# A convolution through two Fourier steps: two pieces of filler work are placed in later half rounds

## The chip, the cores and the metric

The kernel runs on one core of a Trainium2 chip. A core has five engines that work side by side, each through its own queue in program order: TensorE (PE in the profile; matmuls, with PEld for its weight loads), VectorE (DVE), ScalarE (ACT), GpSimd (POOL) and SyncE (SP), which issues the DMAs. Matmuls write into PSUM, eight banks; VectorE and ScalarE carry results from there into SBUF. The metric is the device time of one execution in microseconds (us).

## The reference

```python
# x: (1, 224, 224, 96) bf16, w: (7, 7, 96, 96) bf16
wp = jnp.pad(w, ((0, H - K), (0, W - K), (0, 0), (0, 0)))
Xf = rfft2(x.astype(float32), axes=(1, 2))
Wf = rfft2(wp.astype(float32), axes=(0, 1))
Yf = jnp.einsum('bhwi,hwio->bhwo', Xf, Wf)
y = irfft2(Yf, s=(H, W)).astype(bfloat16)
```

It is a circular 7 x 7 convolution of a 224 x 224 image with 96 channels in and 96 out, written as a product of spectra.

## The kernel before

**What it computes.** The kernel transforms only along the rows' axis h, in 8 blocks of 28 rows that overlap by 6, to 17 frequencies per block (`NS`, slots 0 to 16; slots 0 and 16 hold real parts only). Along the other axis w it stays in the pixel domain and forms two output pixels at a time from fewer products than a plain sum over taps would take.

**Tiles.** The image is cut along w into seven tiles of 32 columns, `t` = 0 to 6 in the code. The third tile is `t` = 2; below, "tile 2" means this. For each tile four kinds of work follow each other:

- the forward transform: matmuls of pixels (`xn`) with a table (`Fm`) into a PSUM bank, and an evacuation into `xf`. There are two such buffers, so tile 2 uses tile 0's again. A copy of three neighbour columns per phase from the previous tile goes before it (`new_xf`, line 432; two ScalarE copies).
- planes: sums and differences of `xf` on VectorE, into `J` (`jit`, line 518), for groups of three slots (`JGB`), three instructions per group.
- rounds: one per slot (`b_round`, line 578). The first product, 19 matmuls into one bank, uses `J` and `xf` as weights' side and the transformed filter `WF`; ScalarE copies a part of it (`tt_`), VectorE forms `u` from the bank and that copy. Then a place for filler work, `mid()`. The second product, 14 matmuls into another bank, from which VectorE forms `v`. GpSimd (in some rounds VectorE) adds u and v into `yf`. Then a second place for filler work, `end()`. The buffers of u and v are two each, so the u of a round waits until GpSimd has added the one of two rounds before. In slots 0 and 16 a round has 8 + 14 matmuls and one VectorE sum.
- the inverse transform: `yf` goes to DRAM (`scr`), comes back in another order (`tt`, `load_t`, line 702), and an inverse job (`c_jobs`, line 762) multiplies it with `Gm`: two matmuls into two banks, two evacuations into `yo` or a free plane buffer, and the output DMA after some of the jobs. A tile has eleven such jobs, on five loads. When a load's last job is done, the next load into its buffer is issued (`pump`).

**Order.** Every engine's order is the order in which the Python code emits the work. Filler work stands in lists: `add(a, b, jobs)` (line 853) spreads jobs evenly over half rounds a to b - 1, and `pace` (line 837) emits as many of them at a `mid()` or `end()` as are due:

```python
due = n if k >= b - 1 else -(-n * (k - a + 1) // (b - a))
while jobs and n - len(jobs) < due:
    jobs.pop(0)()
```

**Tiles 0 and 1** run together, tile 1 four rounds behind tile 0 (line 869, `r` = 0 to 20). While both run (r = 4 to 16), half round 2r is tile 0's round and half round 2r + 1 is tile 1's. Fillers here: filter jobs (`prep_jobs`, line 388: matmuls on `wq` into a bank, evacuated into `WF` by ScalarE, and at the end of each group the differences of `WF` on VectorE), with the last group in half rounds 22 to 26; and tile 2's forward transform in two ranges of slots (`FR2`, line 44; lines 886 to 893): slots 0 to 9 from half round 22 in nine half rounds, 12 jobs (one bank, 5 or 6 matmuls and one evacuation each), and slots 10 to 16 from half round 34 in six, 8 jobs. At the end of the second range the pixels of tile 3 are loaded.

**Tiles 2 to 6** run one by one (line 923). Here half rounds 2s and 2s + 1 are the `mid()` and `end()` of round s. Fillers of tile t: the forward transform of tile t + 1 (24 jobs up to half round 25) and inverse jobs of tile t - 1 or what is left of tile t - 2. In tile 2 these are the eleven jobs of tile 0 (`CQ[2] = (11, 0)`), paced from half round `k0` (line 933) to 33; in the other tiles they start in half round 3. The loads for tile 0's inverse jobs are queued in round r = 20 of the stretch before.

**PSUM.** All banks come from one pool of eight. A bank that a matmul wants must have been emptied by the VectorE or ScalarE instruction that reads it; which bank that is follows from the order of the program. An evacuation goes to VectorE or ScalarE by a running count of each one's load (`evac`); from tile 0's rounds on this puts nearly all of them on ScalarE.

Of the kernel before, what the change touches and what calls it, by code (L numbers as in the profile page):

```python
# [40 lines left out]
CQ = {2: (11, 0), 3: (11, 2), 4: (9, 5), 5: (6, 8), 6: (3, 8)}  # L41
SH2 = (0, 8, 13, 17)
FR0 = (0, 8, 17)
FR2 = ((0, 10, 22, 9), (10, 17, 34, 6))
MERGE = ()
NP2 = 0
FI = 6
# [11 lines left out]
def kernel(  # L59
# [426 lines left out]
    def a_jobs(t):  # L486
        xf = new_xf(t)
        jobs = []
        for jg in range(2):
            for h in range(2):  # L490
                for (q, n) in ((0, 3), (3, 3), (6, 2)):
                    jobs.extend(a_bank(t, xf, xn_bufs[jg], h * PXC + 2 * q, n, jg, HALO + h * 8 + q))
            jobs.append(then_load(jobs.pop(), t + 1, jg))
        return jobs
# [23 lines left out]
    def jit(t, g):  # L518
        s0, s1 = JGB[g]
        n = s1 - s0  # L520
        xf = xf_tiles[t][0:C]
        xv = xf.rearrange("c p r s w j -> c p r s (w j)")
        b = jcount[0] % 3 if t < 2 else (jcount[0] - 2 * len(JGB)) % 2
        jcount[0] += 1
        Jb = J_bufs[b][0:C].rearrange("c (k s q) -> c k s q", k=7, s=3)
        for s in range(s0, s1):
            jbuf[(t, s)] = Jb[:, :, s - s0]

        def sub(o, a, b, op, cost):
            def f():  # L530
                load["v"] += 170 + cost / 1.92
                return VE.tensor_tensor(out=o, in0=a, in1=b, op=op)
            return f
        x0, x1 = xv[:, 0, :, s0:s1], xv[:, 1, :, s0:s1]
        c0, c1 = max(s0, REAL[0] + 1), min(s1, REAL[1])
        i0, i1 = c0 - s0, c1 - s0
        pd, rd, sd, qd = x1.ap
        dpl = bass.AP(x1.tensor, x1.offset - NJ, [pd, [NJ, 2], rd, sd, qd])
        return [
            sub(Jb[:, 0:4, 0:n].rearrange("c (k r) s q -> c k r s q", r=2), dpl,  # L540
                x0.unsqueeze(1).to_broadcast([C, 2, 2, n, PP]), ALU.subtract, 4 * PP * n),
            sub(Jb[:, 4, i0:i1], xv[:, 0, 0, c0:c1], xv[:, 0, 1, c0:c1], ALU.add, PP * (c1 - c0)),
            sub(Jb[:, 5:7, i0:i1], Jb[:, 0:4:2, i0:i1], Jb[:, 1:4:2, i0:i1], ALU.add, 2 * PP * (c1 - c0)),
        ]

    def late_planes(s):
        x0, x1 = (xf_tiles[TL][0:C, ph, :, s].rearrange("c r w j -> c r (w j)") for ph in range(2))
        o = LATE[s]
        Jb = jbuf[(TL, s)] = xs[0:C, o:o + 7 * PP].rearrange("c (k q) -> c k q", q=PP)
        pd, rd, qd = x1.ap  # L550
        dpl = bass.AP(x1.tensor, x1.offset - NJ, [pd, [NJ, 2], rd, qd])

        def sub(o, a, b, op, n):
            def f():
                load["v"] += 170 + n * PP / 1.92
                return VE.tensor_tensor(out=o, in0=a, in1=b, op=op)
            return f
        ops = [sub(Jb[:, 0:4].rearrange("c (k r) q -> c k r q", r=2), dpl, x0.unsqueeze(1).to_broadcast([C, 2, 2, PP]), ALU.subtract, 4)]
        if s not in REAL:
            ops += [sub(Jb[:, 4], x0[:, 0], x0[:, 1], ALU.add, 1), sub(Jb[:, 5:7], Jb[:, 0:4:2], Jb[:, 1:4:2], ALU.add, 2)]  # L560
        return ops
# [167 lines left out]
    def turn_a(i):  # L729
        src = xn_all[:, 0:NA].bitcast(F32).rearrange("p (g k s) -> p g k s", k=2, s=SR)  # L730
        turn(src, xs[:, 0:NA], i * C // 8, (i + 1) * C // 8)
# [30 lines left out]
    def c_jobs(t):  # L762
        jobs = []
        w0 = t * 2 * TW
        for gi, h in LT:
            hold = {}
            nq = 2 if gi < 2 else 3

            def mk_(q, gi=gi, h=h, nq=nq, hold=hold):
                def put(j0, nj, px, npx, row, col):  # L770
                    dma(out[0, j0 * B:(j0 + nj) * B, w0 + px:w0 + px + npx, :].rearrange("h w c -> h (w c)"),
                        hold["yo"][row:row + nj * B, col:col + npx * C])

                def f():
                    if q % 2 == 0:
                        hold["yo"] = new_yo()
                    tt = tt_tiles[(t, gi, h)]
                    yo = hold["yo"]
                    nj = 2 if q == 2 else 3
                    for b in range(2):  # L780
                        pb = bank()[0:3 * B, 0:4 * C]
                        TE.matmul(pb, lhsT=G[0:nj * FR],
                                  rhs=tt[0:nj * FR, 4 * q + 2 * b:4 * q + 2 * b + 2, :].rearrange("p w e -> p (w e)"), start=True, stop=True)
                        k = 2 * (q % 2) + b
                        evac(yo[0:nj * B, k * 4 * C:(k + 1) * 4 * C], pb[0:nj * B], 4 * C)
                    if q == 1 and gi < 2:
                        put(gi * 3, 3, h * PXC, PXC, 0, 0)
                    elif q == 1:
                        put(6, 2, 0, 16, 0, 0)
                        for j in range(2):  # L790
                            put(6 + j, 1, 24, 8, 2 * B, j * 8 * C)
                    elif q == 2:
                        put(6, 2, 16, 8, 0, 0)
                    if q == nq - 1:
                        held[gi == 2] -= 1
                        pump()
                return f
            for q in range(nq):
                jobs.append(mk_(q))
        return jobs  # L800
# [11 lines left out]
    def queue_c(t):  # L812
        pend.extend((t, *k) for k in LT)
        pump()
# [30 lines left out]
    def fills(qs, k):  # L845
        def f():
            for q in qs:
                pace(q, k)
        return f
# [3 lines left out]
    def add(a, b, jobs):  # L853
        qs.append([a, b, jobs, len(jobs)])
# [14 lines left out]
    for r in range(NS + LAG):  # L869
# [5 lines left out]
        for p in range(3):  # L875
            if r == (1, 3, 5)[p]:
# [8 lines left out]
                add(2 * r + 1, 2 * r + (5, 5, 4)[p], fj[0] + fj[1])  # L885
        for s0, s1, k0, n in FR2:
            if 2 * r == k0:
# [35 lines left out]
    for t in range(2, NT):  # L923
        if t == TL:
            GE.memset(YA[:, :, 2 * SA:, :].rearrange("p g s o -> p g (s o)"), 0.0)
        else:
            scr_tiles[t] = dr_pool.tile([TW, NJ, NS, 4 * C], BF16, name="scr")
        qs = []
        if t + 1 < NT:
            add(4 if t == 2 else 0, 26, a_jobs(t + 1))  # L930
        nold, nnew = CQ[t]
        k1 = 2 * NS if t < TL else 2 * NS - 2
        k0 = 10 if t == 2 else 3
        km = 14 if t == TL else k0 + -(-(k1 - k0) * nold // (nold + nnew))
        add(k0, km, cj[:nold])
        cn = c_jobs(t - 1)
        cj = cn[nnew:]
        add(km, k1, cn[:nnew])
        plan = {}
        for g, (s0, s1) in enumerate(JGB):  # L940
            if g + 1 < len(JGB) - (t == TL) or t + 1 < NT:
                plan[s0 if g + 1 < len(JGB) else s0 - 1] = g
        for s in range(NS):
            now = ()
            if s in plan:
                g = plan[s]
                now = jit(t, g + 1) if g + 1 < len(JGB) else jit(t + 1, 0)
            if s == 3:
                queue_c(t - 1)
            if t in (3, 4):  # L950
                next(gp, None)
            mid = fills(qs, 2 * s)
            if t == TL and s in LROUND:
                now = late_planes(LROUND[s])
            if t == TL and s >= SA:
                if s < NS - 1:
                    now = [lambda i=s - SA: turn_a(i)]
                else:
                    mid = lambda m=mid: (m(), turn_a(3))
            b_round(t, s, mid, fills(qs, 2 * s + 1), bool(now) and t != TL, now)  # L960
# [70 lines left out]
```

## Time and profile before

| | |
|---|---|
| median of 3 runs | 257.67 us (257.16 to 257.9) |
| the profiled execution | 257.39 us, span 255.7 us |
| granted TensorE clock | 0.998 |
| TensorE busy | 245.9 us (96%), 5015 matmuls |
| VectorE busy | 214.5 us (84%) |
| ScalarE busy | 201.6 us (79%) |
| GpSimd busy | 108.4 us (42%) |
| chain that ended last | TensorE 82%, DMA 7%, VectorE 4% |

All instructions carry line 92, the helper that records the order, so rows are told apart by tiles: `pb<-WF,J` and `pb<-WF,xf` are products, `pb<-wq` filter jobs, `pb<-Fm,xn` forward transforms (80 columns per matmul in tile 2's first range, 56 in its second, 136 in later tiles), `pb<-tt,Gm` inverse jobs. A row of a timeline gives the start in us, the duration in us, the engine and line, the operation, its tiles, and in brackets the idle time of the engine before it with what ended that. Rows of equal instructions are merged; the end of a row of matmuls is modelled and overlaps the next row, so starts are the better measure. Tile 0 and 1's rounds end near 92 us, tile 2's at 121, tile 3's at 152.

### The profile page before, as it was taken

To read this page: it belongs to the slowest core of one execution; us is meant where nothing else is said; L and a number is where in the kernel's file an instruction comes from. 1 tells how busy PE (TensorE), PEld (TensorE's weight loads), DVE (VectorE), ACT (ScalarE), POOL (GpSimd) and SP (SyncE) were. 2 spreads that over 40 slices of the span, in tenths; PEclk is the share of its full clock that TensorE was granted. 3 is DMA by queue.
4 is the path that set the end of the run, shared out by engine and by line. 5 is a ranking of instruction groups with operands and counts; after the bars stand their busy time and mean duration, and the time that the engine had idled before them with its cause. 6 is when DMAs were issued, how large, how long until landed. Compare 5 with 4: busy or idle time off the path is not lost.

```text
span 255.7 us, 11925 instructions
## 1 busy us (share of the span) xinstructions
PE 245.9 (96%) x5015; PEld 231.5 (91%) x5015; DVE 214.5 (84%) x463; ACT 201.6 (79%) x499; POOL 108.4 (42%) x174
## 2 busy tenths in 40 slices
PE   8989999999999999999999999999999999999981
PEld 3789999999999998999999989999999999999971
DVE  6999899899788987779788896788978889989982
ACT  7889978586973877997988879888897976567762
POOL 7885514354446535331433324433243332464721
PEclk9999999999999999999999999999999999999999
DMA  7963103711111569887989559697959853496145
GB/s 170 244 184 93 43 9 91 233 49 49 49 49 53 175 187 158 241 234 233 283 247 227 168 154 313 195 271 189 322 209 207 258 169 104 137 172 177 54 121 178
DMA packets 41511, 42.80 MB, mean 167 GB/s; under 512 B 30836, under 2 KB 33072, under 8 KB 41458
## 3 DMA queue, kind: packets, MB, share of 16 engines
q1 hardware_dynamic: 41140, 41.36, 58.5%
q8 instruction: 39, 0.64, 1.0%
q0 software_dynamic: 192, 0.52, 0.7%
q10 hardware_dynamic: 126, 0.17, 0.2%
q14 instruction: 14, 0.11, 0.1%
HBM read 22.37 MB, written 19.66 MB: 164 GB/s over the span
## 4 chain that ended last, share of the span: by engine, by line
PE 82%; DMA 7%; DVE 4%; issue 2%; ACT 2%; SPq 1%; POOL 0%; DVEq 0%
PE pb L92 82%; DMA tt<-scr 2%; DMA WF<-in_x_dram 2%; DMA wq<-in_w_dram 2%; SPq L92 1%; ACT xf L92 1%; DVE xf L92 1%; DVE J L92 1%; DVE WF L92 1%; DVE v L92 1%; DVE u L92 0%; POOL yf L92 0%; ACT tt L92 0%; ACT WF L92 0%; ACT ct L92 0%
## 5 line engine op out<-in xcount | busy, mean ns | idle before, releaser
L92 PE MATMUL pb<-WF,J 96*128 96x96 bf16 x2782 | 160.3, 206 | 0.5 <-DVE u L92 0.4
L92 PEld LDWEIGHTS <-J 96*128 96x128 bf16 x2782 | 136.8, 98 | 7.3 <-issue 0.7
L92 POOL TENSOR_TENSOR yf<-v,u 128x384 bf16<-128x384 f32 x70 | 69.6, 1010 | 119.3 <-issue 64.1
L92 ACT CAST xf<-pb 96x408 bf16<-96x408 f32 (+8 forms) x145 | 67.5, 488 | 3.9 <-PE pb L92 1.8
L92 PE MATMUL pb<-WF,xf 96*128 96x96 bf16 x991 | 61.5, 206 | 0.7 <-ACT xf L92 0.4
L92 DVE TENSOR_TENSOR J<-xf 96x1824 bf16<-96x1824 bf16 (+1 forms) x82 | 56.0, 722 | 0.1
L92 PEld LDWEIGHTS <-xf 96*128 96x128 bf16 x991 | 48.9, 98 | 1.4 <-ACT xf L92 0.6
L92 PE MATMUL pb<-Fm,xn 118*128 118x136 bf16 (+5 forms) x576 | 44.4, 203 | 0.0
L92 PE MATMUL pb<-tt,Gm 102*84 102x384 bf16 (+1 forms) x132 | 32.0, 325 | 0.5 <-DMA tt<-scr 0.5
L92 ACT CAST yo<-pb 84x384 bf16<-84x384 f32 (+1 forms) x65 | 27.8, 484 | 3.3 <-PE pb L92 3.3
L92 ACT CAST J<-pb 84x384 bf16<-84x384 f32 (+1 forms) x65 | 28.0, 486 | 2.2 <-PE pb L92 2.2
L92 ACT CAST WF<-pb 96x480 bf16<-96x480 f32 (+1 forms) x59 | 29.0, 562 | 0.7 <-PE pb L92 0.6
L92 PEld LDWEIGHTS <-xn 118*128 118x128 bf16 x576 | 29.0, 97 | 0.3
L92 DVE TENSOR_TENSOR J<-J 96x912 bf16<-96x912 bf16 (+2 forms) x41 | 22.6, 551 | 0.0
L92 PE MATMUL pb<-wq 128*128 128x120 bf16 (+1 forms) x288 | 21.7, 226 | 0.5 <-ACT wq L92 0.5
L92 PEld LDWEIGHTS <-wq 128*128 128x128 bf16 x288 | 19.7, 149 | 1.0 <-ACT wq L92 0.9
L92 POOL TENSOR_TENSOR xn<-v,u 128x384 bf16<-128x384 f32 x12 | 10.9, 923 | 8.9 <-DVE J L92 5.9
L92 PEld LDWEIGHTS <-Gm 102*84 102x84 bf16 (+1 forms) x132 | 11.4, 118 | 0.8 <-issue 0.6
L92 DVE TENSOR_TENSOR yf<-v,u 128x384 bf16<-128x384 f32 x20 | 11.3, 567 | 0.8 <-DMA scr<-yf 0.2
L92 ACT COPY xf<-xf 96x816 bf16<-96x816 bf16 (+4 forms) x16 | 9.9, 675 | 0.0
L92 DVE TENSOR_TENSOR WF<-WF 96x960 bf16<-96x960 bf16 x14 | 9.4, 719 | 0.1
L92 PE MATMUL pb<-wu 128*128 128x512 bf16 x26 | 8.1, 479 | 1.1 <-DVE ct L92 1.1
(410 smaller groups left out, 255.0 us busy)
## 6 DMA issues: line engine op xcount, KB each, us to landing
scr<-yf SPq DMA_DIRECT2D x30, 288.0 KB
xn<-in_x_dram SPq DMA_DIRECT2D x12, 672.0 KB
tt<-scr SPq DMA_DIRECT2D x24, 336.0 KB
out_dram<-yo SPq DMA_DIRECT2D x12, 252.0 KB
out_dram<-J SPq DMA_DIRECT2D x12, 252.0 KB
tt<-scr SPq DMA_DIRECT2D x6, 288.0 KB
scr<-yf SPq DMA_DIRECT2D x6, 192.0 KB
WF<-in_x_dram SPq DMA_DIRECT2D x2, 343.0 KB
```

What stands on the lines that cost most here:

```text
L92: r = fn(*a, **k)
```

## The change

Tile 2's first range (slots 0 to 9) moves from half rounds 22 to 30 into half rounds 24 to 33: the neighbour copies are emitted at r = 12 in place of 11, and the 12 jobs are spread over ten half rounds in place of nine. The eleven inverse jobs in tile 2's rounds are spread over half rounds 12 to 33 in place of 10 to 33. No job is added or taken away.

```diff
-FR2 = ((0, 10, 22, 9), (10, 17, 34, 6))
+FR2 = ((0, 10, 24, 10), (10, 17, 34, 6))
...
         nold, nnew = CQ[t]
         k1 = 2 * NS if t < TL else 2 * NS - 2
-        k0 = 10 if t == 2 else 3
+        k0 = 12 if t == 2 else 3
         km = 14 if t == TL else k0 + -(-(k1 - k0) * nold // (nold + nnew))
         add(k0, km, cj[:nold])
```

In the order of the built program this moves, besides the matmuls on TensorE and their evacuations on ScalarE, some DMA issues on SyncE: the load of tile 4's first pixels goes ahead of the first output DMA and the first reload, and two writes of `yf` to DRAM go ahead of an output. The order of instructions on VectorE and GpSimd is the same as before.

## The prediction

> **What bounds the kernel now.** I read the page's busy shares first, then the chain that ended last, then the timelines of TensorE, VectorE and ScalarE around the places where that chain leaves TensorE.
>
> ```profile
> PE 245.9 (96%) x5015; PEld 231.5 (91%) x5015; DVE 214.5 (84%) x463; ACT 201.6 (79%) x499; POOL 108.4 (42%) x174
> PE 82%; DMA 7%; DVE 4%; issue 2%; ACT 2%; SPq 1%; POOL 0%; DVEq 0%
> ```
>
> TensorE is the bound: only its gaps can be saved, and every new gap costs its full length. In the stretches below matmuls follow each other at a fixed pitch, start to start: 42.5 ns for a product matmul (18 in 0.76 us), 36 ns for an 80-column transform matmul (10 in 0.36), 60 ns for a 136-column one (3 in 0.18), 63 ns for a filter matmul (12 in 0.76). Between 28 us and the last tile the chain leaves TensorE at three places. The timeline of TensorE around the first:
>
> ```profile
> 61.51 0.92 PE L92 MATMUL pb<-wq 128*128 128x120 bf16 x12
> 62.27 0.76 PE L92 MATMUL pb<-Fm,xn 118*128 118x80 bf16 x12
> 62.91 0.93 PE L92 MATMUL pb<-WF,J 96*128 96x96 bf16 x18
> ...
> 65.08 0.34 PE L92 MATMUL pb<-Fm,xn 118*128 118x80 bf16 x5
> 65.81 0.93 PE L92 MATMUL pb<-WF,J 96*128 96x96 bf16 x18 [0.39 <-DVE u L92]
> ```
>
> Half round 22 starts its fills at 61.51, half round 23 at 64.31. Five transform matmuls from 65.08 take 0.18, so TensorE stands from 65.26 to 65.81: 0.55 us (the row's 0.39 counts from a modelled end). Twelve from 62.27 should take 0.43 but take 0.64: another 0.20. The cause is VectorE's queue:
>
> ```profile
> 59.83 2.31 DVE L92 TENSOR_TENSOR WF<-WF 96x960 bf16<-96x960 bf16 x3
> 62.06 0.54 DVE L92 SCALAR_TENSOR_TENSOR v<-tt__1756,pb 128x384 f32<-128x384 f32 x1
> ...
> 63.25 1.70 DVE L92 TENSOR_TENSOR J<-xf 96x1824 bf16<-96x1824 bf16 x2
> 64.87 0.62 DVE L92 TENSOR_TENSOR J<-J 96x912 bf16<-96x912 bf16 x1
> 65.42 0.34 DVE L92 SCALAR_TENSOR_TENSOR u<-pb,tt__1849 128x192 f32<-128x192 f32 x1
> 65.68 0.54 DVE L92 SCALAR_TENSOR_TENSOR v<-tt__1849,pb 128x384 f32<-128x384 f32 x1
> 66.66 0.36 DVE L92 SCALAR_TENSOR_TENSOR u<-pb,tt__1926 128x192 f32<-128x192 f32 x1 [0.44 <-POOL yf L92]
> ```
>
> Three filter differences and a group of planes stand in front of u and v, which empty PSUM banks. Half rounds 22 and 23 take 7 and 6 of the 8 banks (two products, three filter jobs, two and one transform jobs), so TensorE soon needs a bank that VectorE still holds. The second and third place, in the same view of TensorE, with the load from the chain:
>
> ```profile
> 92.87 6.32 DMA tt<-scr
> ```
>
> ```profile
> 98.50 0.34 PE L92 MATMUL pb<-Fm,xn 118*128 118x136 bf16 x3
> 99.32 0.49 PE L92 MATMUL pb<-tt,Gm 102*84 102x384 bf16 x2 [0.48 <-DMA tt<-scr]
> ...
> 151.47 0.76 PE L92 MATMUL pb<-WF,J 96*128 96x96 bf16 x14
> 152.53 0.50 PE L92 MATMUL pb<-WF,xf 96*128 96x96 bf16 x8 [0.30 <-DVE u L92]
> ```
>
> 98.50 plus 0.18 is 98.68, and the next start is 99.32: the first inverse job, in half round 10, waits 0.64 for its load. 151.47 plus 14 x 42.5 ns is 152.06: 0.47 at the border from tile 3 to tile 4. At the border from tile 2 to tile 3 (121.02) there is none.
>
> **Part 1: the transform's first range, half rounds 24 to 33.** No work is added: 64 matmuls and 12 evacuations (12 x 0.45 to 0.5 us) move, with two copies of neighbour columns (1.08 us together, ScalarE, at 60.60). All evacuations stay on ScalarE; VectorE's and GpSimd's order stays as it was. The range issues no DMA; the load of tile 3's pixels hangs on the second range, which stays.
>
> VectorE's times up to u of half round 23 do not depend on the moved work: v(21) ends at 63.32, the planes at 65.49, u(22) at 65.76, v(22) at 66.22, u(23), held by GpSimd, at 67.02. TensorE, from 61.51, by the pitches: filter jobs to 62.27, second product of 22 (0.60) to 62.86, first of 23 (0.81) to 63.67, filter jobs to 64.43, second product to 65.02, first of 24 to 65.83 (its planes are ready at 65.49), filter jobs, the second of which now needs v(22): 66.09 to 66.27, a wait of 0.18; they end at 66.76. The two transform jobs of half round 24 need u(23): at 67.07, a wait of 0.30; to 67.48; second product to 68.08. Half round 25 then needs 0.81 + 0.76 + 0.18 + 0.60: 70.42. Before, it ended at 71.26 (70.66 + 0.60) with 32 transform matmuls done, now with 17; the 15 others cost 0.54 later. Saved: 71.26 - 70.42 - 0.54 = **0.30**.
>
> The cover further on: u(24) must be done by 68.89. ScalarE, which now meets the two copies between the dense half rounds, ends half round 23's three filter evacuations at 66.0, the copies at 67.1, the copy that u(24) reads at 67.4; GpSimd frees u's buffer at 67.6; u(24) ends at 68.0. That leaves 0.9 us, and it is 0.3 earlier than before (68.34). After that VectorE runs ahead, since in the trace of before it idles 3.1 us between 66 and 80 (0.44, 0.50, 0.60, 0.75, 0.44, 0.35), and half rounds 31 to 33, empty of fills until now, hold 4 of the 12 jobs while VectorE works without a pause from 80.16 to 86. They take 3 banks each in place of 2; the last needed early, u(29), ends near 77.9 for a start at 79.4.
>
> Ends: +0.75 if neither wait comes back, -0.61 if the same release still stood in front and the 17 matmuls that covered it (0.61) came on top. As built, the bank that TensorE needs there is a later one and more work stands before it, so I take the worked 0.30.
>
> **Part 2: the first inverse job in half round 12.** Eleven jobs (two matmuls, 0.33 us, and two evacuations, 0.74, each), their output DMAs and the reloads of their buffers start two half rounds later and go at every second half round in place of every 2.18. Half round 10 loses its 0.33 and the wait. The second product of half round 10 starts at 99.65 - 0.33 - 0.64 = 98.68; it, the transform job, the next first product and another transform job (0.60 + 0.18 + 0.81 + 0.18) end at 100.45, less part 1's 0.30 at 100.15. There the job of half round 12 finds a load that landed at 99.2, 0.9 us before, or 1.2 if it comes 0.30 earlier as its issue does. Its other two waits, u and v of round 4, end near 99.6 and 100.1. Saved: **0.64** (ends: 0 if the load slipped to 100.8, and 0.64).
>
> [...]
>
> SyncE's queue: tile 4's first pixel loads go ahead of the first output and reload, two writes of the intermediate likewise ahead of an output. Nobody waits for outputs; the reloads serve tile 3, whose first inverse job comes at 124, and were issued from 109.5: over 10 us of cover against a slip of about 2. ScalarE between half rounds 12 and 25, per round: 0.31 + 2.2 x 0.36 + 0.74 = 1.84 us, against TensorE's 1.40 + 0.35 + 0.33 = 2.08: covered by 0.24.
>
> At the end the last jobs move from half rounds 29 and 31 into 28, 30 and 32, the middles of rounds 14 to 16, as tile 3 has them in 30 and 32. As built, the first product of tile 3 then waits for u of round 15, like tile 4's at 152.53. VectorE ends that u 4.0 us after round 14's first product (117.43 to 121.42; 148.48 to 152.47), 4.15 here, since v(14) has to follow the later second product. TensorE gets there after 0.33 + 0.60 + 0.81 + 0.33 + 0.60 + 0.34 + 0.33 + 0.60 = 3.94 (tile 3, one job fewer: 3.58). With 0.06 for the signal: a new wait of about **0.30** (ends: 0, and the 0.59 that tile 4's border loses in all, 0.47 and 0.12 before 152.99).
>
> Sum: 0.30 + 0.64 - 0.30 = 0.64 saved. The profiled execution took 257.39 (span 255.7); it would take 256.75. The median of runs, 0.28 above it, gives 257.67 - 0.64 = **257.03**.
>
> **Rivals.** (a) No wait comes back: 0.30 to 0.75 and 0.64, no loss at the border: 0.94 to 1.39, 256.28 to 256.73. For it: ScalarE and VectorE both run earlier through the dense half rounds. Against it: the program's bank waits at the border.
> (b) The waits only move: part 1 gives 0, the border costs 0.59, and 0.05 is left: 257.62; without the load's gain 258.3. For it: VectorE's queue is unchanged, and it is what TensorE waited for.
> (c) Slower: ScalarE's copies. They stood in a pause of ScalarE (it idles 0.99 before and 1.03 after them) and come to stand behind six evacuations. If u(24) ends later than 68.89, every us is lost by TensorE in full; 1.08 us of copies beyond the 0.9 of cover, with the later jobs shifted behind them, could take up to 1.1, and with part 1 at -0.61: 257.67 + 1.1 + 0.61 + 0.30 - 0.64 = 259.0; near 258.5 where half of it comes. Against it: the rows put u(24) at 68.0. The Trainium skill, "PSUM — Partial Sum Buffer", section "Engine vs sequencer instructions", says that ScalarE's queue is strictly first in, first out, which is how this would come about; the trace agrees, its 499 rows of ScalarE stand in the program's order.
>
> **How the numbers follow.** The forecast (0.3 to 1.0 saved, 256.7 to 257.4) 0.50, (a) 0.20, (b) 0.17, (c) 0.13. 0.3% is 0.77 us, about what can be told from no change: below 256.90 lie (a) and 0.15 of the forecast: 0.35. Above 258.44 lies (c) and little of (b): 0.14. Between: 0.51. The range 256.4 to 258.1 leaves out (c) and the far end of (a).
>
> **What would show it.** Right: no wait at 65.8, two short ones for VectorE near 66.1 and 66.8; no wait for the load near 98.7; a new one for u at tile 3's first product, near 120. Wrong: a wait longer than 0.6 in half rounds 24 or 25, ScalarE as its releaser, or TensorE waiting anywhere between 70 and 83.

## The result and the profile after

The changed kernel takes 256.84 us (median of 22 runs, 256.28 to 257.48), the kernel before, on the same chip, 257.38 (median of 22 runs; the three runs known at the time of the prediction had given 257.67). The ratio is 0.9975, with a 95% interval of 0.9964 to 0.9986: 0.64 us saved of 257.38, between 0.36 and 0.93. The means of the runs (256.80 and 257.45) lie 0.65 apart, the medians 0.54.

The profiled execution of the changed kernel took 257.48 us with a span of 255.8, no less than the one of before (257.39, 255.7). Its half round 22 began at 61.96 in place of 61.51, and what follows tile 4's first product took 0.17 longer (103.32 for 103.15). The change moves no work of TensorE in either stretch, and among the ten profiles shown here half round 22 begins anywhere from 60.97 to 61.96. What the change does is therefore read inside the span, between marks that both profiles have. Busy shares and the chain's shares, from the page:

```profile
PE 246.6 (96%) x5015; PEld 231.7 (91%) x5015; DVE 215.1 (84%) x463; ACT 201.1 (79%) x499; POOL 107.9 (42%) x174
PE 87%; DMA 5%; ACT 2%; issue 2%; DVE 1%; SPq 1%; POOL 0%; DVEq 0%
```

TensorE is as busy as before; its share of the chain went from 82 to 87%, and DMA's from 7 to 5%: the load is off the chain. The chain, in order of time (start, duration, what), now leaves TensorE between 67 us and tile 4 only here:

```profile
67.13 0.37 DVE u L92
67.50 0.04 issue
67.54 53.27 PE pb L92 x1186
...
120.85 0.05 DVE u L92
120.90 0.04 issue
120.94 31.21 PE pb L92 x629
...
152.19 0.21 DVE u L92
```

The timeline of TensorE at the three places where the prediction had something to happen (start, duration, operation; in brackets idle time and what ended it):

```profile
66.31 1.05 PE L92 MATMUL pb<-wq 128*128 128x120 bf16 x12
67.54 0.60 PE L92 MATMUL pb<-Fm,xn 118*128 118x80 bf16 x12 [0.18 <-DVE u L92]
...
69.38 0.96 PE L92 MATMUL pb<-wq 128*128 128x120 bf16 x12
70.18 0.34 PE L92 MATMUL pb<-Fm,xn 118*128 118x80 bf16 x5
70.36 0.93 PE L92 MATMUL pb<-WF,J 96*128 96x96 bf16 x18
...
100.52 0.34 PE L92 MATMUL pb<-Fm,xn 118*128 118x136 bf16 x3
100.70 0.49 PE L92 MATMUL pb<-tt,Gm 102*84 102x384 bf16 x2
...
120.04 0.76 PE L92 MATMUL pb<-WF,J 96*128 96x96 bf16 x14
120.94 0.50 PE L92 MATMUL pb<-WF,xf 96*128 96x96 bf16 x8
```

At half round 24, twelve filter matmuls from 66.31 should end at 67.07, and the transform starts at 67.54: one gap of 0.47 us in place of the two of before, 0.20 and 0.55. The first inverse job starts at 100.70, right behind the three transform matmuls (100.52 plus 0.18): the wait of 0.64 for the load is gone. Tile 3's first product starts at 120.94 where the row ahead of it ends at 120.04 plus 0.60: a new wait of 0.30. VectorE, ScalarE and GpSimd around half round 24:

```profile
63.23 0.53 DVE L92 SCALAR_TENSOR_TENSOR v<-tt__1802,pb 128x384 f32<-128x384 f32 x1
63.70 1.70 DVE L92 TENSOR_TENSOR J<-xf 96x1824 bf16<-96x1824 bf16 x2
65.32 0.62 DVE L92 TENSOR_TENSOR J<-J 96x912 bf16<-96x912 bf16 x1
...
66.14 0.54 DVE L92 SCALAR_TENSOR_TENSOR v<-tt__1847,pb 128x384 f32<-128x384 f32 x1
67.13 0.36 DVE L92 SCALAR_TENSOR_TENSOR u<-pb,tt__1908 128x192 f32<-128x192 f32 x1 [0.46 <-POOL yf L92]
...
68.09 0.36 DVE L92 SCALAR_TENSOR_TENSOR u<-pb,tt__1971 128x192 f32<-128x192 f32 x1
```

```profile
66.44 1.13 ACT L92 COPY xf<-xf 96x480 bf16<-96x480 bf16 x2
```

```profile
63.12 1.01 POOL L92 TENSOR_TENSOR yf<-v,u 128x384 bf16<-128x384 f32 x1 [2.20 <-DVE v L92]
66.08 1.02 POOL L92 TENSOR_TENSOR yf<-v,u 128x384 bf16<-128x384 f32 x1 [1.95 <-issue]
67.07 1.00 POOL L92 TENSOR_TENSOR yf<-v,u 128x384 bf16<-128x384 f32 x1
```

With the 0.45 us by which this profile runs late taken off, u of half round 23 ends at 67.04 (predicted 67.02), ScalarE's copies at 67.12 (67.1) and u of half round 24 at 68.00 (68.0).

Three stretches of TensorE, start to start, serve for all comparisons below: A from the first filter job of half round 22 to the start of half round 34 (0.81 us, a first product, ahead of the first 56-column transform row), B from there to tile 3's first product, C from there to tile 4's first product. C, which nine of the ten kernels leave alone, is 31.50 or 31.51 in all nine.

| kernel | A | B | C | sum | ratio of times to before, 95% |
|---|---|---|---|---|---|
| before | 21.67 | 37.84 | 31.51 | 91.02 | 1 |
| the changed kernel | 21.47 | 37.51 | 31.50 | 90.48 | 0.9975 (0.9964 to 0.9986) |
| part 1 alone | 21.44 | 37.86 | 31.50 | 90.80 | 0.9985 (0.9969 to 1.0002) |
| part 2 alone | 21.69 | 37.70 | 31.50 | 90.89 | 0.9998 (0.9983 to 1.0012) |
| inverse jobs ended by half round 31, tile 2 | 21.47 | 37.21 | 31.50 | 90.18 | 0.9961 (0.9945 to 0.9978) |
| the same for tiles 2 and 3 | 21.45 | 37.21 | 31.04 | 89.70 | 0.9942 (0.9927 to 0.9956) |
| copies twice | 21.75 | 37.50 | 31.50 | 90.75 | 0.9983 (0.9962 to 1.0004) |
| copies in their old place | 21.47 | 37.50 | 31.50 | 90.47 | 0.9978 (0.9966 to 0.999) |
| before, differences spread | 22.01 | 38.39 | 31.51 | 91.91 | 1.0028 (1.0004 to 1.0052) |
| before, two differences left out | 20.93 | 37.40 | 31.51 | 89.84 | one run, 256.45 us |

The change saves 0.20 in A, 0.33 in B and nothing in C: 0.54 us.

### The profile page after: what moved, and what is told of

Same layout as the page of the kernel before. It is cut to its first block, busy times and chain, and to the rows that moved or that the text cites. A ratio compares the mean times of both kernels' runs of the same rounds, so it can differ in the third digit from the quotient of the medians.

```text
span 255.8 us, 11924 instructions
## 1 busy us (share of the span) xinstructions
PE 246.6 (96%) x5015; PEld 231.7 (91%) x5015; DVE 215.1 (84%) x463; ACT 201.1 (79%) x499; POOL 107.9 (42%) x174
## 4 chain that ended last, share of the span: by engine, by line
PE 87%; DMA 5%; ACT 2%; issue 2%; DVE 1%; SPq 1%; POOL 0%; DVEq 0%
PE pb L92 87%; DMA WF<-in_x_dram 2%; DMA wq<-in_w_dram 2%; SPq L92 1%; ACT xf L92 1%; DVE xf L92 1%; POOL yf L92 0%; ACT tt L92 0%; DVE u L92 0%; DVE v L92 0%; ACT WF L92 0%; ACT ct L92 0%; ACT tt__688 L92 0%; DVEq L92 0%
## 5 line engine op out<-in xcount | busy, mean ns | idle before, releaser
L92 PE MATMUL pb<-wu 128*128 128x512 bf16 x26 | 8.7, 509 | 1.1 <-DVE ct L92 1.1
```

The source lines that it names most:

```text
L92: r = fn(*a, **k)
```

## The experiments

### Each part alone

```diff
-FR2 = ((0, 10, 22, 9), (10, 17, 34, 6))
+FR2 = ((0, 10, 24, 10), (10, 17, 34, 6))
```

> The first edit alone (range in half rounds 24 to 33, inverse jobs from half round 10 as before). Theory: the waits for VectorE in half rounds 22 and 23 (0.20 + 0.55) are replaced by 0.18 + 0.30 in half round 24, so from the filter jobs of half round 22 to the start of half round 34 TensorE needs 21.4 to 21.5 us in place of 21.67 (0.2 to 0.3 saved, ratio 0.999); the wait for the load, 0.64, stays; no wait at tile 3's first product. Rival (the waits only move): 21.67 and ratio 1.000. Rival (all the gain of the change is the load's wait): the same.

Measured: 257.07 us against 257.43 of before, 0.9985 (0.9969 to 1.0002), which does not reach past no change. The profile is sharper: A is 21.44, 0.23 shorter. In B the wait for the load is all there; TensorE's timeline:

```profile
98.12 0.34 PE L92 MATMUL pb<-Fm,xn 118*128 118x136 bf16 x3
98.96 0.49 PE L92 MATMUL pb<-tt,Gm 102*84 102x384 bf16 x2 [0.50 <-DMA tt<-scr]
```

The wait is 0.66 where before it was 0.64. So the two parts act in separate stretches, and part 1 does nothing for the load.

```diff
-        k0 = 10 if t == 2 else 3
+        k0 = 12 if t == 2 else 3
```

> The second edit alone (inverse jobs from half round 12, the range from half round 22 as before). Theory: the waits of 0.20 and 0.55 stay, the 0.64 for the load goes, a new wait of 0.30 for u at tile 3's first product; 0.34 saved, ratio 0.9987. Rival (the border wait comes from both edits together): no wait at the border, 0.64 saved, 0.9975. Rival (the load is late for half round 12 too without the first edit): a wait remains, under 0.2 saved.

Measured: 257.42 us, 0.9998 (0.9983 to 1.0012); the expected saving lies inside the interval, and so does none. In the profile the wait for the load is gone and the wait of 0.30 at tile 3's first product is there, both as expected; but B is only 0.14 shorter, since a gap that neither kernel had stands here, in TensorE's timeline:

```profile
102.70 0.96 PE L92 MATMUL pb<-WF,J 96*128 96x96 bf16 x14
103.50 0.52 PE L92 MATMUL pb<-Fm,xn 118*128 118x136 bf16 x6
```

Fourteen product matmuls from 102.70 should end at 103.30, and the transform starts 0.20 later. The profile names no releaser. The transform's matmuls are the first on the second half of tile 3's pixels, but a late load is not the reason: the semaphores that they wait for are complete at 97.5 in the same trace, and the gap lies inside the row of products, behind the eleventh. None of the other nine profiles has it, and its cause is open. The rival that the load of `tt` would be late here too falls: it landed at 98.90, and the job starts at 100.40.

### What is behind the new wait at the border

The changed kernel, with tile 2's inverse jobs spread over half rounds 12 to 31. By `pace` the last of them then falls in half round 30, the middle of round 15, and no filler stands in the middle of round 16, the last one:

```diff
-        k1 = 2 * NS if t < TL else 2 * NS - 2
+        k1 = 2 * NS - 2 if t in (2, TL) else 2 * NS
```

> Both edits, and tile 2's eleven inverse jobs end at half round 31 (spread over 12 to 31), so that none stands in the middle of round 16. Theory: the border wait of 0.30 goes, nothing else changes: about 0.3 faster than the change, 0.8 to 0.9 against before, ratio 0.9966. Rival (the border wait is VectorE's lag whatever stands in round 16): the wait stays, ratio 0.9975.

Measured: 256.38 us, 0.9961 (0.9945 to 0.9978). The wait at tile 3's first product is 0.01 and B is 37.21, 0.30 shorter than with the change as made. A and C are as with the change as made, so nothing was paid there for packing the eleven jobs closer. The new wait is thus made by the place of the last inverse job, and it is the 0.30 that part 2 gives back.

### Is it VectorE's queue that made the first two waits?

Two runs on the kernel before. The first spreads the three filter differences of the fourth group, one each in half rounds 20, 21 and 22, to let u and v of half round 22 through earlier:

```diff
-        add(2 * PGRP[gi - 1][0], 2 * PGRP[gi - 1][1] - 1, prep_jobs(gi))
+        a0, b0 = 2 * PGRP[gi - 1][0], 2 * PGRP[gi - 1][1] - 1
+        pj = prep_jobs(gi)
+        if gi == 4:
+            add(a0, b0 - 1, pj[:12])
+            add(b0 - 1, b0 + 2, pj[12:])
+        else:
+            add(a0, b0, pj)
...
```

> The kernel before, with the three filter differences of the fourth group spread over half rounds 20, 21 and 22 instead of all three in 20. Theory (VectorE's queue holds the banks): u of half round 22 ends 0.7 earlier, both waits (0.20 and 0.55) go, 0.6 to 0.75 saved, ratio 0.997 to 0.9975, with the range where it was. Rival (the banks are short because filter and transform jobs are too dense, whatever VectorE's order): the waits stay, ratio 1.000.

A miss: 257.92 us, 1.0028 (1.0004 to 1.0052), slower by the times, though two of the twelve runs (260.26 and 260.29) make up over half of that. The profile shows it without them: A is 22.01, with waits of 0.30, 0.39 and 0.44 in it. The differences got longer; VectorE's timeline, and GpSimd's of the same kernel:

```profile
59.61 1.17 DVE L92 TENSOR_TENSOR WF<-WF 96x960 bf16<-96x960 bf16 x1
...
61.43 1.43 DVE L92 TENSOR_TENSOR WF<-WF 96x960 bf16<-96x960 bf16 x1
...
65.39 1.45 DVE L92 TENSOR_TENSOR WF<-WF 96x960 bf16<-96x960 bf16 x1
```

```profile
58.30 1.96 POOL L92 TENSOR_TENSOR yf<-v,u 128x384 bf16<-128x384 f32 x2 [1.95 <-issue]
61.32 1.03 POOL L92 TENSOR_TENSOR yf<-v,u 128x384 bf16<-128x384 f32 x1 [1.06 <-DVE v L92]
65.33 0.99 POOL L92 TENSOR_TENSOR yf<-v,u 128x384 bf16<-128x384 f32 x1 [2.98 <-issue]
```

GpSimd's sums end at 60.26, 62.35 and 66.32; the differences end at 60.78, 62.86 and 66.84, that is 0.52, 0.51 and 0.52 later, however long before they had started. A difference makes no headway while GpSimd's sum runs. Three in a row behind one sum took 2.31 in the kernel before; one behind each of three sums took 4.05. The run could not answer its question, since the work it meant to spread grew by 1.74 us. Its B is 0.55 longer as well, by a wait of 1.19 for the load.

The second run takes two of the three differences out and leaves all other instructions near there as they were:

```diff
     def diff(s):
         def f():
             load["v"] += 60 + C * NTAP / 1.92
+            if s in (12, 13):
+                return
...
+        if r == 5:
+            for sl in (slot(12, 2), slot(13, 2)):
+                GE.memset(WF[0:C, sl].rearrange("i t o -> i (t o)"), 0.0)
```

> The kernel before, leaving out the filter differences of slots 12 and 13 on VectorE (their places are filled with zeros by GpSimd much earlier, so those two slots' products come out with zeros): 2 x 0.77 us less in VectorE's queue just ahead of v of half round 21, and no other instruction moved on any engine near there. Theory: VectorE's queue is what TensorE waits for at half rounds 22 to 24; u and v of half round 22 end 1.5 us earlier, both waits (0.20 and 0.55) go, and the stretch from half round 22 to 34 takes 20.9 to 21.1 in place of 21.67. Rival: what holds the banks is the number of fills or ScalarE's evacuations, and VectorE is only named because it comes last; then at least 0.4 of the 0.75 stays, 21.3 or more.

Measured: A is 20.93, shorter by 0.74, which is the sum of the two waits (0.75). TensorE, and VectorE:

```profile
62.50 0.60 PE L92 MATMUL pb<-Fm,xn 118*128 118x80 bf16 x12
62.94 0.93 PE L92 MATMUL pb<-WF,J 96*128 96x96 bf16 x18
...
65.10 0.34 PE L92 MATMUL pb<-Fm,xn 118*128 118x80 bf16 x5
65.28 0.93 PE L92 MATMUL pb<-WF,J 96*128 96x96 bf16 x18
```

```profile
60.03 1.17 DVE L92 TENSOR_TENSOR WF<-WF 96x960 bf16<-96x960 bf16 x1
...
64.52 0.34 DVE L92 SCALAR_TENSOR_TENSOR u<-pb,tt__1849 128x192 f32<-128x192 f32 x1
64.79 0.54 DVE L92 SCALAR_TENSOR_TENSOR v<-tt__1849,pb 128x384 f32<-128x384 f32 x1
```

Twelve transform matmuls take 0.44 to the next start where they took 0.64, and five take 0.18 where 0.73 passed. The fills are as many and ScalarE's work is the same, so the rival falls: VectorE's queue was what TensorE waited for. (B is 0.44 shorter in this profile, since only 0.06 of the wait for the load is left; that was not followed further.) One number was missed: u and v of half round 22 come 1.1 us earlier against the start of half round 22, not 1.5, because the one difference that is left still sits behind GpSimd's sum and takes 1.17.

### ScalarE's copies in the dense half rounds

Rival (c) was tested from both sides. On the changed kernel, the two copies of neighbour columns issued twice:

```diff
             if 2 * r == k0:
                 new_xf(2, s0, s1)
+                if s0 == 0:
+                    la = load["a"]
+                    new_xf(2, s0, s1)
+                    load["a"] = la
                 fj = f_jobs(2, s0, s1)
```

> The changed kernel with the two neighbour copies of the first range issued twice, one pair behind the other: 1.08 us more of ScalarE between the dense half rounds 23 and 24, nothing else moved. In the profile of the changed kernel u of half round 24 ends at 68.45 and TensorE needs it near 69.34 (0.9 of cover). Theory: the second pair eats that cover and little more, 1.08 - 0.9 = 0.2 us lost, up to 0.4 with later jobs shifted; from half round 22 to 34 the stretch takes 21.7 to 21.9 in place of 21.47, and the time is 0.9983 to 0.9991 of the kernel before. Rival (c), that there is no cover and ScalarE's copies set the pace there: the full 1.08 is lost, 22.5 us in the stretch, 1.0017 of the kernel before.

Measured: 257.15 us, 0.9983 (0.9962 to 1.0004). The rival's 1.0017 lies outside the interval, but the times alone do not tell this kernel from the changed one; A does: 21.75, 0.28 longer than with single copies, as the theory had it and far from 22.5. ScalarE, VectorE and TensorE of this kernel:

```profile
66.25 2.12 ACT L92 COPY xf<-xf 96x480 bf16<-96x480 bf16 x4
```

```profile
68.77 0.36 DVE L92 SCALAR_TENSOR_TENSOR u<-pb,tt__1973 128x192 f32<-128x192 f32 x1 [1.04 <-ACT tt__1973 L92]
```

```profile
69.18 0.90 PE L92 MATMUL pb<-wq 128*128 128x120 bf16 x12
69.92 0.34 PE L92 MATMUL pb<-Fm,xn 118*128 118x80 bf16 x5
...
71.51 0.34 PE L92 MATMUL pb<-Fm,xn 118*128 118x80 bf16 x5
71.75 0.41 PE L92 MATMUL pb<-WF,J 96*128 96x96 bf16 x6
...
74.10 0.62 PE L92 MATMUL pb<-WF,xf 96*128 96x96 bf16 x8
74.56 0.46 PE L92 MATMUL pb<-WF,J 96*128 96x96 bf16 x7
```

The copies take 0.99 longer in all, u of half round 24 now waits for ScalarE and ends at 69.13, against the start of half round 22 0.89 later than in the changed kernel. TensorE's fills of half round 25 start at 69.18 without a gap: the cover of 0.9 was there and is now used up. The 0.28 is lost behind it, 0.06 at 71.75, 0.12 at 74.56 and 0.11 near 82.

The other side: the copies back in ScalarE's pause at r = 11, the jobs where the change put them.

```diff
+        if r == 11:
+            new_xf(2, 0, 10)
         for s0, s1, k0, n in FR2:
             if 2 * r == k0:
-                new_xf(2, s0, s1)
+                if s0:
+                    new_xf(2, s0, s1)
```

> The changed kernel with the neighbour copies of the first range left where they stood before (r = 11, in ScalarE's pause), the twelve jobs in half rounds 24 to 33 as changed. Theory: the copies are covered in either place, so the stretch from half round 22 to 34 stays within 0.05 of 21.47 and the time within 0.0005 of the changed kernel's 0.9975 of before. Rival (c): the copies in the dense stretch cost part of what the move gains; then the stretch is 0.1 to 0.3 shorter (21.2 to 21.4) and the time 0.9963 to 0.9971.

Measured: 256.74 us, 0.9978 (0.9966 to 0.999), and A is 21.47, equal to the hundredth. GpSimd and VectorE of this kernel:

```profile
66.43 1.01 POOL L92 TENSOR_TENSOR yf<-v,u 128x384 bf16<-128x384 f32 x1
```

```profile
67.47 0.36 DVE L92 SCALAR_TENSOR_TENSOR u<-pb,tt__1971 128x192 f32<-128x192 f32 x1
```

Against the start of half round 22 (61.34 here), u of half round 24 ends at 6.49 in both: it starts when GpSimd has freed its buffer (at 67.44 here, at 68.07 in the changed kernel, where u starts at 68.09), and ScalarE's copies end before that. The copies' new place costs nothing, and rival (c) falls.

### A version faster than both

On the changed kernel, the inverse jobs of both tile 2 and tile 3 ended by half round 31. The text below speaks of the last two rounds, but in both tiles a job still stands in the middle of round 15; only the middle of round 16 is free:

```diff
-        k1 = 2 * NS if t < TL else 2 * NS - 2
+        k1 = 2 * NS - 2 if t in (2, 3, TL) else 2 * NS
```

> The changed kernel with the inverse jobs of tile 2 and of tile 3 ended in half round 31 in place of 33, so that no filler stands in the middle of the last two rounds before either border (before, tile 3 had them there and tile 4's first product waited 0.47 for u). Ending tile 2's alone took the wait of 0.30 away and gave 0.9961 of the kernel before, against 0.9975 for the change as made. Theory: the same now happens at tile 4's border, where the wait of 0.47 and the 0.12 behind it go; another 0.4 to 0.6 us, 0.9938 to 0.9946 of the kernel before. Rival: the eleven jobs of tile 3, now closer together, meet ScalarE or the reloads and give the gain back; 0.996 or more.

Measured: 255.83 us (255.62 to 256.09), 0.9942 (0.9927 to 0.9956). TensorE at the two borders:

```profile
119.44 0.76 PE L92 MATMUL pb<-WF,J 96*128 96x96 bf16 x14
120.04 0.50 PE L92 MATMUL pb<-WF,xf 96*128 96x96 bf16 x8
...
150.48 0.76 PE L92 MATMUL pb<-WF,J 96*128 96x96 bf16 x14
151.08 0.50 PE L92 MATMUL pb<-WF,xf 96*128 96x96 bf16 x8
```

Both next products start 0.60 after the row before them, which is its 14 matmuls and nothing else. C is 31.04, 0.46 shorter: the wait of 0.47 at tile 4's border is gone, and with it the 0.12 behind that product, which lies outside C. The sum of the three stretches is 89.70, 1.32 below the kernel before and 0.78 below the change as made.

## Why the prediction was right, point by point

**The total.** Predicted 257.03 for 257.67, a ratio of 0.9975; measured 0.9975. That the two agree to the last digit is luck: the medians and the profiles' three stretches put the saving at 0.54 where the working had 0.64, and the interval is wider than that difference. The medians are both lower than the numbers of the prediction because more runs of before gave 257.38. No row of TensorE waits between 70 and 83, as the prediction's last lines asked.

**Part 1.** The mechanism held: the ends of VectorE's instructions up to u of half round 23 did not depend on the moved work and came within 0.02 of the predicted ones, and leaving two differences out showed that its queue was the cause of both old waits. The two short waits (0.18 and 0.30) appear as one gap of 0.47 to 0.48, since the merged row of filter matmuls hides the first. Their sum is right. The saving was 0.20 (0.23 alone) and not 0.30: half round 25 ended at 70.36 + 0.60 - 0.45 = 70.51 for a predicted 70.42. The step mis-sized is the sum over half rounds 24 and 25 by pitches alone: the transform of 24 started at 67.54 - 0.45 = 67.09 for 67.07 and took 0.43 for 0.41, the filter jobs of 25 took 0.80 for 0.76, and the rest is rounding. (The first product of 24 took 0.84 for 0.81, which the waits behind it absorbed.) One count was wrong, without effect: half rounds 31 to 33 hold three of the twelve jobs, not four. The cover for u of half round 24 was 0.9 as worked out; the run with doubled copies used it to within 0.05.

The working took as given that GpSimd frees the buffer of u of half round 23 late, and did not ask why. Its sum for half round 21 starts at 66.08 after 1.95 of idle, though the v that it reads had ended at 63.76 and GpSimd was free at 64.13. The kernel makes the sum of a round with planes wait for the last of them (`pool_sum`, line 688), and the planes end at 65.94. So VectorE's block sets the second short wait too, through GpSimd, and by the program's choice; no run takes that dependency out.

**Part 2.** Both terms are right: 0.64 gained at the load, 0.30 lost at the border, 0.33 in B in the changed kernel. What the steps did not have is the gap of 0.20 that part 2 alone met in the stretch behind, whose cause is open. The load's cover was put at 0.9 to 1.2 us. In the changed kernel's trace the load was issued at 91.90 and its semaphore is complete at 99.21, 1.49 before the job at 100.70. In the six profiles with the job in half round 12 the cover is between 0.43 (copies in their old place: 99.64 for a job at 100.07) and 2.19 (inverse jobs ended by half round 31 in tile 2: 97.52 for 99.71), and in all ten the load took 5.9 to 8.4 us. So the cover held each time, once with only 0.43 left: the load's 6.32 in the profile of before was one value from a wide spread.

**The rivals.** (a) failed in half round 24, where 0.47 of waiting came back, and at the border, where the wait came as the rows of tile 4's border had shown it. (b) failed in part 1 because the moved work met VectorE's unchanged queue later, so that 0.75 of waiting became 0.48, and in part 2 because the border cost half of what the load's wait had. (c) failed because u of half round 24 is released by GpSimd, after ScalarE's copies are done.

**What the prediction left unused.** It named the border's wait as a price and took tile 4's wait as given. Both have the same cause, the filler in the middle of a tile's last round, and taking it away at both borders took the ratio from 0.9975 to 0.9942 (0.78 us in the three stretches), more than the change itself had gained.

## What to carry to other kernels

Where an in-order engine empties the banks, put filler that needs banks behind the moment at which that engine is through its own block of work; the waits shrink to what is left of the block, and a table of ends of that engine's instructions gives the remainder to a few hundredths. Before a border between two stages, keep fillers out of the middle of the last round: there the next stage's first step needs the results at once, and a filler that costs nothing elsewhere delays them. When a gain is a few tenths of a us, compare stretches between marks inside the span, since head and tail of two profiles can differ by more than that.

## What was not expected of the hardware

VectorE's filter differences (two SBUF inputs) stand still while a GpSimd sum runs. In four rows of two kernels (59.61, 61.43 and 65.39 with spread differences; 60.03 with two left out, where GpSimd's sums ended at 60.69 and the difference at 61.20) the difference ended 0.51 to 0.52 after GpSimd's sum, whether it had started 0.65 or 0.93 us before that; differences that no sum overlaps took 0.64 or 0.65 in the same traces. The Trainium skill, "Trainium Architecture — The Big Picture", section "What this means for kernel authors", says that the port pair shared by VectorE and GpSimd is an exclusive lock and not a split of bandwidth; the trace agrees, with these numbers. That these instructions wait for that lock, and not for something else that GpSimd holds, was only read from the rows.

The same load of `tt` landed between 5.9 and 8.4 us after its issue in the ten profiles, of kernels whose work up to there differs little (6.3 before, 7.3 in the changed kernel, 7.55 with part 1 alone). Such a load wants more cover than one profile suggests.
